# One DMA transpose for the probabilities of a pair of units instead of two, in a block-sparse attention with a feed-forward layer

## The chip, the core and the metric

The kernel runs on one core of one Trainium2 chip. The metric is the time of one execution on the device in microseconds (us); lower is better. A core has TensorE (PE in the profile, with its weight loads as PEld), VectorE (DVE), ScalarE (ACT), GpSimd (POOL) and SyncE (SP). SP computes nothing: it is the engine that issues this kernel's DMAs, one after the other in program order. Sixteen DMA engines then move the data.

## The reference

Attention over 4 batches, 8 heads, 768 positions and a head size of 64, with a mask of 32x32 blocks; then one feed-forward layer over the 3072 tokens.

```
scores = q @ k^T / sqrt(64)                       # [4, 8, 768, 768]
mask   = |block_i - block_j| <= 1, or block_i or block_j is the first or last block,
         or block_j is one of three sampled blocks of block_i
attn   = softmax(where(mask, scores, -1e9))
x      = (attn @ v) as [3072, 512]
h      = x @ w_in                                 # [3072, 2048]
out    = max(0.01 * h, h) @ w_out                 # [3072, 512]
```

## The kernel before

**Tiling.** Two blocks of queries (64 rows) make a tile `T`; there are 12 tiles in a batch. Only the keys that the mask allows are gathered: 12 slots of 32 keys, so 384 keys (`KEYS`) for a tile. A *unit* is one tile with two heads (64 query rows of the one and of the other fill the 128 partitions); a *pair* is two units with neighbouring `hp`, so four heads of one tile. Tile 0 of each batch (the first and the last query block) sees all 768 keys, and its units have two `parts` of 384 keys; all other units have one. That makes 192 units, 96 pairs and 208 parts. Four tiles (256 tokens) make an *item*, and once an item's attention is done its feed-forward layer runs in 8 chunks: `ffn_h` (lines 739 to 751, matmuls at L749), the leaky ReLU on ACT, DVE and POOL (L756, L760, L765, L766) and `ffn_o` (L768 to 784, matmuls at L779). TensorE multiplies in fp16; values are split into a high and a low half, and products are summed over halves.

**One unit.** `scores` (L651) multiplies queries and gathered keys into PSUM; `unit_ttr` (L658, DVE) adds the mask and takes the row's extreme; `unit_exp` (L669, ACT) makes the exponentials in a float32 buffer `p`. `pair_norm` (L677, L678) makes the two reciprocals `r` of a pair. `unit_high` (L684, ACT) writes the high half of the probabilities to a buffer `pp`, `unit_split` writes the low half (L689, DVE) and has SP transpose the buffer by a DMA into `pt` (L692). `pair_av` (L714) multiplies both units' `pt` with the values into `av`; it takes the pair's second unit first. `pp` and `pt` each have six buffers of one part; a counter (`tlive`) makes `split_step` emit a pair's `pair_av` before a seventh `pt` would be needed.

**The queue.** All DMAs are issued by SP: queries (`rq`), their transpose (L535, `qs`) and the exchange of its halves (L537, L538, `qxs`), keys (`rk`) and their transpose (L512, `kt`, a buffer of 128x1536 fp16 elements that comes out as 12 blocks of 128x128), values, the scratch copy of the values (`scr`), and for each tile the gather of its values into one of two buffers `vg` (L611 to L621: six of the rows' addresses are read by SP itself from a table, L619). `pt<-pp` transposes 128x768 elements, 6 blocks; `qs<-qa` 128x1024, 8 blocks.

**What sets the order.** The loop over `units` (L1027 to 1126) emits the steps with priorities; a scheduler then lays all engines' instructions out by its own model of their times and of when buffers come free. Each engine executes its list strictly in that order and waits on semaphores where data or a buffer is not ready. So a change to one instruction moves others all over the program.

Of the kernel before, what the change touches and what calls it, by code (L numbers as in the profile page):

```python
# [11 lines left out]
F16 = mybir.dt.float16  # L12
# [7 lines left out]
P = 128  # L20
# [8 lines left out]
KEYS = SLOTS * BLOCK  # L29
CFG = {  # L30
    "ahead": 3,
    "av_lag": 3,
    "bs": 1500,
    "early": 2,
    "flag": 1,
    "g": 2,
    "g_at": 0,
    "ht": 1,
# [5 lines left out]
    "ob": 4,  # L44
    "ord": "dtsixScmgovabphw",
    "p": 4,
    "pp": 6,
    "pt": 6,
    "rq": 1,
    "q_at": 8,  # L50
    "rk": 2,
# [14 lines left out]
def tile_block_sparse_attention_ffn(  # L66
# [19 lines left out]
    nc = tc.nc  # L86
# [13 lines left out]
    NCH = KEYS // P  # L100
# [6 lines left out]
    pa = ctx.enter_context(tc.tile_pool(name="pa", bufs=2))  # L107
# [571 lines left out]

    def unit_high(u):  # L680
        u.r = u.pair.r[:, u.pi:u.pi + 1]
        u.pp = [pa.tile([P, 2, KEYS], F16, tag="pp", name=f"pp_{u.nm}_{i}", bufs=CFG["pp"]) for i in range(u.parts)]
        for p, pp in zip(u.p, u.pp):
            nc.scalar.activation(pp[:, 0, :], p, AF.Copy, scale=u.r)  # L684

    def unit_split(u):
        u.pt = []
        for i, (p, pp) in enumerate(zip(u.p, u.pp)):
            nc.vector.scalar_tensor_tensor(  # L689
                out=pp[:, 1, :], in0=p, scalar=u.r, in1=pp[:, 0, :], op0=ALU.mult, op1=ALU.subtract)  # L690
            pt = pa.tile([P, 2, NCH, P], F16, tag="pt", name=f"pt_{u.nm}_{i}", bufs=CFG["pt"])
            nc.sync.dma_start_transpose(  # L692
                out=pt.rearrange("p l c t -> p (l c) t"), in_=pp.rearrange("p l t -> p (l t)"))
            u.pt.append(pt)

    avs = {}

    def pair_av(pr):

        if pr.hp == 0:  # L700
            avs[pr.item.n, pr.T] = bank(f"av_{pr.nm}", "av").rearrange("p (n l t) -> p n l t", n=NP, l=2)
        pr.av = avs[pr.item.n, pr.T]
        for u in pr.units:
            require_v(u.b, u.hp, u.T)
        emits = []
        for u in pr.units[::-1]:
            n = NCH * u.parts
            for c in range(n):
                for l in range(2):
                    for hh in range(2):  # L710
                        vt = vgs[u.b, u.T][:, c, 2 * u.hp + hh, :] if u.T else v16s[u.b, u.hp][:, c, hh, :]
                        emits.append(lambda o=pr.av[hh * D:(hh + 1) * D, u.hp], a=vt[:, l * D:(l + 1) * D],
                                     m=u.pt[c // NCH][:, :, c % NCH, hh * D:(hh + 1) * D], c=c, l=l, n=n:
                                     nc.tensor.matmul(o, a, m, start=(c == 0 and l == 0), stop=(c == n - 1 and l == 1)))  # L714
        together(emits)

    def tile_evac(pr):

        it = pr.item
        tmp = pf.tile([P, NP, Q2], F32, tag="avt", name=f"avt_{pr.nm}", bufs=1)  # L720
        nc.scalar.activation(tmp, pr.av[:, :, 1, :], AF.Copy, scale=1.0 / PSCALE)
        yield
        xf = pf.tile([P, NP, Q2], F32, tag="xf", name=f"xf_{pr.nm}", bufs=1)
        nc.vector.scalar_tensor_tensor(
            out=xf, in0=pr.av[:, :, 0, :], scalar=1.0 / PSCALE, in1=tmp, op0=ALU.mult, op1=ALU.add)
        yield
        if it.x is None:
            it.x = pa.tile([P, 2, NP, N2], F16, tag="x", name=f"x_{it.nm}", bufs=CFG["xbufs"])
        xs = it.x[:, :, :, pr.k * Q2:(pr.k + 1) * Q2]
        nc.scalar.activation(xs[:, 0], xf, AF.Copy)  # L730
        yield
        nc.gpsimd.tensor_tensor(out=xs[:, 1], in0=xf, in1=xs[:, 0], op=ALU.subtract)  # L732
        it.nx += 1
# [78 lines left out]
    for b in range(B):  # L812
        for j in range(NI):
# [3 lines left out]
            for k_ in range(TPI):  # L817
                for hp in range(0, NP, 2):
                    pr = Unit()
                    pr.item, pr.k, pr.T, pr.hp, pr.nm, pr.units = it, k_, j * TPI + k_, hp, f"{it.nm}_{k_}_{hp}", []  # L820
                    for pi in range(2):
                        u = Unit()
# [171 lines left out]
    def high_step():  # L994
        if pend_high:
            unit_high(pend_high[0])
            pend_split.append(pend_high.popleft())

    tlive = [0]

    def split_step():
        if pend_split:
            pu = pend_split.popleft()
            while tlive[0] + pu.parts > CFG["pt"]:
                av_step(True)
            tlive[0] += pu.parts
            unit_split(pu)
            live[0] -= pu.parts
            if pu.pi == 1:
                pend_av.append((step + CFG["av_lag"], pu.pair))  # L1010

    def av_step(now=False):
        if pend_av and (now or pend_av[0][0] <= step):
            pr = pend_av.popleft()[1]
            tlive[0] -= 2 * pr.units[0].parts
            while evs and pr.hp == 0:
                ev_step()
            pair_av(pr)
            if pr.hp == NP - 2:
                vfree[0] += pr.T > 0  # L1020
                evs.append(tile_evac(pr))

    def ev_step():
        if evs and next(evs[0], "end") == "end":
            evs.pop(0)

    for u in units:  # L1027
# [9 lines left out]
        if nb < B:  # L1037
            g = it.j * 16 + ui
            t = g - (CFG["k_at"] if b else CFG["k_at0"])
# [5 lines left out]
            t = g - CFG["v_at"]  # L1045
# [17 lines left out]
        c = aq[0] if aq else None  # L1063
        for w in CFG["ord"]:
# [19 lines left out]
            elif w == "t":  # L1084
                while live[0] + u.parts > CFG["p"]:
                    if not pend_high and not pend_split:
                        norm_step()
                    high_step()
                    split_step()
# [6 lines left out]
            elif w == "d":  # L1096
                norm_step()
            elif w == "i":
                high_step()
            elif w == "s":  # L1100
                split_step()
            elif w == "a":
                av_step()
                if vq and vfree[0] and (vq[0][0], "ready") in scr:
                    start_gather_v()
            elif w == "v":
                ev_step()
            elif w == "b":
                do_out()
            elif w == "o":  # L1110
                do_o(CFG["flag"] if hq or aq else 0)
            elif w == "p":
                side_step(CFG["side0"] if step < 16 else CFG["side"])
                gather_step(2)
            elif w == "w":
                wcredit += [r for a, r in CFG["wr"] if step >= a][-1]
                while wcredit >= 1.0:
                    c = next(weights, "end")
                    wcredit -= c if c != "end" else wcredit
            elif w == "h":  # L1120
                for i in range(n):
                    if i:
                        do_act()
                        do_o(CFG["flag"])
                    do_h()
# [3 lines left out]
    while pend_norm or pend_high or pend_split or pend_av or evs:  # L1129
        ev_step()  # L1130
        av_step()
        split_step()
        norm_step()
        high_step()
        if step in ready:
            add_ffn(ready.pop(step))
        do_h()
        do_act()
        do_o(CFG["flag"])
        do_out()  # L1140
        step += 1
# [49 lines left out]
```

## Time and profile before

| what | value |
|---|---|
| time before, median of 3 runs | 943.82 us (943.46 to 947.15) |
| the profiled execution, first to last instruction | 944.7 us |
| TensorE, share of the span busy | 80% |
| DVE, ACT, POOL | 64%, 52%, 35% |
| mean granted TensorE clock | 0.931 of full speed |
| DMA issues of `pt<-pp` | 208 |

The profile is of one execution, and its span stands for that execution's own time: 0.9 us above the median of the runs. The execution has four stages. Up to 60 us the inputs and the first weights arrive; from 60 to 213 us the weights are decoded and split while the first attention units run; from 213 to about 860 us attention and feed-forward chunks run side by side; after 860 us the last items' feed-forward layers are left. The views name a line as L714 and a DMA as `pt<-pp` (what it writes and reads). SP's instructions are sequencer instructions: the profile has their start and length, and counts no busy time for the engine.

### The profile page before, as it was taken

How to read it: one execution, taken by the hardware profiler on the slowest of the kernel's cores; microseconds unless marked ns; L12 is line 12 of the kernel's file. 1: busy time of each engine (PE TensorE's matmuls, PEld its weight loads, DVE VectorE, ACT ScalarE, POOL GpSimd, SP SyncE). 2: the span in 40 equal slices, each digit the busy share in tenths (PEclk: the TensorE clock that was granted, in tenths of full speed). 3: DMA queues.
4: the chain of work that ended last, by engine and by line, in shares of the span. 5: the costliest groups of instructions: out<-in, count | busy, mean ns of one | idle time of the engine just before them, and what ended most of it. 6: DMA issues, size and time to landing. Idle time of an engine off the chain costs nothing. (4 is left out here: it accounts for less than half of the span.)

```text
span 944.7 us, 21784 instructions
## 1 busy us (share of the span) xinstructions
PE 754.8 (80%) x7020; PEld 492.8 (52%) x7020; DVE 609.1 (64%) x1643; ACT 488.1 (52%) x1063; POOL 331.3 (35%) x469
## 2 busy tenths in 40 slices
PE   1325456788978979979897968989888988989998
PEld 1214334465645645646554635556455655656674
DVE  4989899996857667557565565567466655745221
ACT  4565768575535456456455554456355554535121
POOL 0234665542215344243324242333323433532221
PEclk9998557799989989999999998999999999989999
DMA  9996798678685767766675978676785665555200
GB/s 209 283 276 162 162 244 187 164 148 167 141 180 128 160 121 157 160 137 130 151 165 111 171 134 147 151 146 127 151 161 125 137 136 139 120 113 123 32 23 23
DMA packets 336624, 139.38 MB, mean 148 GB/s; under 512 B 299389, under 2 KB 311678, under 8 KB 336510
## 3 DMA queue, kind: packets, MB, share of 16 engines
q1 hardware_dynamic: 336510, 137.99, 68.5%
q8 instruction: 55, 0.90, 0.4%
q14 instruction: 59, 0.48, 0.2%
HBM read 65.57 MB, written 12.58 MB: 83 GB/s over the span
## 5 line engine op out<-in xcount | busy, mean ns | idle before, releaser
L779 PE MATMUL o<-W,g 128*128 128x512 f16 x1152 | 279.1, 388 | 7.6 <-ACT ob L797 2.9
L749 PE MATMUL h<-x,W 128*128 128x256 f16 x2304 | 280.9, 279 | 0.3 <-DVE ht L760 0.3
L749 PEld LDWEIGHTS <-W 128*128 128x128 f16 x2304 | 227.2, 101 | 50.7 <-issue 10.5
L766 POOL TENSOR_TENSOR g<-ht,g 128x512 f16<-128x512 f32 x96 | 115.3, 1201 | 336.5 <-DVE g L765 201.2
L689 DVE SCALAR_TENSOR_TENSOR pp<-p,r,pp 128x384 f16<-128x384 f32 x208 | 142.5, 702 | 106.0 <-ACT pp L684 104.4
L779 PEld LDWEIGHTS <-g 128*128 128x128 f16 x1152 | 108.8, 100 | 137.4 <-issue 23.9
L669 ACT ACTIVATE p<-p,mx 128x384 f32<-128x384 f32 x208 | 125.8, 606 | 96.3 <-DVE mx L658 67.0
L591 POOL COPY kg<-kt 128x256 f16 x264 | 129.3, 510 | 131.6 <-PE s L651 74.9
L684 ACT ACTIVATE pp<-p,r 128x384 f16<-128x384 f32 x208 | 119.6, 607 | 103.9 <-DMA pt<-pp 72.0
L714 PE MATMUL av<-pt,vg 128*64 128x128 f16 x2112 | 83.0, 231 | 50.5 <-DMA pt<-pp 40.3
L658 DVE CUSTOM_DVE_ANT_0 p<-s,em,nsc 128x384 f32<-128x384 f32 x176 | 101.9, 609 | 21.1 <-PE s L651 20.0
L714 PEld LDWEIGHTS <-vg 128*64 128x64 f16 x2112 | 72.1, 116 | 77.0 <-issue 57.4
L760 DVE SCALAR_TENSOR_TENSOR ht<-h,gd,ht 128x512 f32<-128x512 f32 x80 | 59.8, 747 | 56.0 <-ACT ht L756 55.7
L756 ACT ACTIVATE ht<-h,gs 128x512 f32<-128x512 f32 x80 | 54.0, 675 | 63.9 <-PE h L749 48.7
L651 PE MATMUL s<-kg,qs_q 128*64 128x384 f16 x352 | 65.1, 364 | 12.1 <-DVE mx L658 7.7
L732 POOL TENSOR_TENSOR x<-xf,x 128x256 f16<-128x256 f32 x48 | 35.8, 745 | 90.7 <-ACT x L730 90.0
L651 PE MATMUL s<-kg,qxs_q 128*64 128x384 f16 x352 | 63.9, 357 | 4.3 <-DMA qxs_q<-qs_q 4.3
L651 PEld LDWEIGHTS <-qs_q 128*64 128x64 f16 x416 | 27.9, 116 | 68.7 <-issue 45.4
L523 ACT ACTIVATE qa_q<-rq 128x512 f16<-128x512 f32 x25 | 15.7, 628 | 68.9 <-DMA rq<-in_q_dram 68.9
L765 DVE CAST g<-ht 128x512 f16<-128x512 f32 x96 | 43.4, 452 | 8.9 <-PE o L779 7.5
L677 DVE TENSOR_SCALAR sum<-sum 128x2 f32<-128x2 f32 x96 | 24.9, 259 | 37.1 <-ACT p L669 36.1
L669 ACT ACTIVATION_READ_ACCUMULATOR p<-p,mx 128x1 f32 x208 | 38.9, 187 | 0.0
(126 smaller groups left out, 726.0 us busy)
## 6 DMA issues: line engine op xcount, KB each, us to landing
vg<-scr SPq DMA_DIRECT2D x280, 64.0 KB, 1.9
vg<-scr SPq DMA_DIRECT2D x44, 256.0 KB, 3.1
v<-in_v_dram SPq DMA_DIRECT2D x32, 192.0 KB, 3.4
qxs_q<-qs_q SPq DMA_DIRECT2D x48, 128.0 KB, 3.0
scr<-v SPq DMA_DIRECT2D x16, 384.0 KB, 3.7
W<-in_moe_w_in_dram SPq DMA_DIRECT2D x5, 1024.0 KB, 5.9
rq<-in_q_dram SPq DMA_DIRECT2D x20, 256.0 KB, 3.5
out_dram<-ob SPq DMA_DIRECT2D x20, 256.0 KB, 2.3
```

The costliest lines, as they stand in the source:

```text
L591: nc.gpsimd.tensor_copy(out=kg[:, :, slot * BLOCK:(slot + 1) * BLOCK], in_=kt[:, :, bass.ds(off, BLOCK)])
L651: nc.tensor.matmul(o, a, k, start=(n == 0), stop=(n == 1)))
L658: nc.vector.tensor_tensor_reduce(out=u.p[i], in0=u.sp[i], in1=kgs[u.b, u.T][1] if u.T else zero.to_broadcast([P, KEYS]), scale=u.nsc, scal ...
L669: nc.scalar.activation(u.p[i], u.p[i], AF.Exp, scale=-1.0, bias=u.mx[:, :1], accum_out=u.pair.sum[:, u.pi, i:i + 1])
L684: nc.scalar.activation(pp[:, 0, :], p, AF.Copy, scale=u.r)
L689: nc.vector.scalar_tensor_tensor(out=pp[:, 1, :], in0=p, scalar=u.r, in1=pp[:, 0, :], op0=ALU.mult, op1=ALU.subtract)
L714: nc.tensor.matmul(o, a, m, start=(c == 0 and l == 0), stop=(c == n - 1 and l == 1)))
L749: nc.tensor.matmul(c.ph[:, i], w, x, start=(d == 0 and m == 0), stop=(d == NP - 1 and m == 2)))
L756: nc.scalar.activation(c.t, c.ph, AF.Copy, scale=scale[1])
L760: nc.vector.scalar_tensor_tensor(out=c.t, in0=c.ph, scalar=scale[0], in1=c.t, op0=ALU.mult, op1=ALU.max)
L766: nc.gpsimd.tensor_tensor(out=c.g[:, 1], in0=c.t, in1=c.g[:, 0], op=ALU.subtract)
L779: nc.tensor.matmul(o, a, w, start=(c.first and i == 0 and m == 0), stop=(c.last and i == 1 and m == 2)))
```

## The change

A pair gets one buffer `pp` that holds both units' probabilities (or, for tile 0, one unit its two parts), and one `pt`; the number of buffers falls from six of one size to three of twice the size. The low half is still written by one DVE instruction for each part, but the DMA is issued only once, after the pair's second unit (or, for tile 0, after the unit's second part), and transposes 128x1536 elements. The counter of `pt` buffers counts by the new size. Everything else in the source is the same. In the built program 208 transposes `pt<-pp` of 6 blocks become 104 of 12 blocks.

```diff
-    "pp": 6,
-    "pt": 6,
+    "pp": 3,
+    "pt": 3,
...
     def unit_high(u):
         u.r = u.pair.r[:, u.pi:u.pi + 1]
-        u.pp = [pa.tile([P, 2, KEYS], F16, tag="pp", name=f"pp_{u.nm}_{i}", bufs=CFG["pp"]) for i in range(u.parts)]
+        if u.parts == 2 or u.pi == 0:
+            u.pair.pp = pa.tile([P, 2, 2, KEYS], F16, tag="pp", name=f"pp_{u.nm}", bufs=CFG["pp"])
+        u.pp = [u.pair.pp[:, i if u.parts == 2 else u.pi] for i in range(u.parts)]
+        u.pp2 = u.pair.pp
         for p, pp in zip(u.p, u.pp):
             nc.scalar.activation(pp[:, 0, :], p, AF.Copy, scale=u.r)
 
     def unit_split(u):
-        u.pt = []
-        for i, (p, pp) in enumerate(zip(u.p, u.pp)):
+        for p, pp in zip(u.p, u.pp):
             nc.vector.scalar_tensor_tensor(
                 out=pp[:, 1, :], in0=p, scalar=u.r, in1=pp[:, 0, :], op0=ALU.mult, op1=ALU.subtract)
-            pt = pa.tile([P, 2, NCH, P], F16, tag="pt", name=f"pt_{u.nm}_{i}", bufs=CFG["pt"])
-            nc.sync.dma_start_transpose(
-                out=pt.rearrange("p l c t -> p (l c) t"), in_=pp.rearrange("p l t -> p (l t)"))
-            u.pt.append(pt)
+        if u.parts == 1 and u.pi == 0:
+            return
+        pt = pa.tile([P, 2, 2, NCH, P], F16, tag="pt", name=f"pt_{u.nm}", bufs=CFG["pt"])
+        nc.sync.dma_start_transpose(
+            out=pt.rearrange("p a l c t -> p (a l c) t"), in_=u.pp2.rearrange("p a l t -> p (a l t)"))
+        if u.parts == 2:
+            u.pt = [pt[:, 0], pt[:, 1]]
+        else:
+            for w in u.pair.units:
+                w.pt = [pt[:, w.pi]]
```

In `split_step` and `av_step` the counter `tlive` goes up by one for each new buffer and down by the pair's number of parts, where it counted parts before.

How the built programs differ is shown at two places, around the pair of units `2_2_0` and `2_2_1` of the third item of batch 1. The names are buffers with their unit (`pt_2_2_1` belongs to the third item, its third tile, unit 1) and a number of the program's own. First SP's list before; this stretch is what SP does from 670.6 to 679.3 us in the profile:

```order
L535 DMA_TRANSPOSE qs_q_0_0_8266<-qa_q_0_0_7938 128x8x128
L473 DMA rq_0_1_8271<-in_q_dram 128x8x64
L692 DMA_TRANSPOSE pt_2_2_0_0_8277<-pp_2_2_0_0_8173 128x6x128
L537 DMA qxs_q_0_0_8268<-qs_q_0_0_8266 64x1024
L538 DMA qxs_q_0_0_8268<-qs_q_0_0_8266 64x1024
L453 DMA scr_8209<-v_2_0_7644 128x6x256
L692 DMA_TRANSPOSE pt_2_2_1_0_8354<-pp_2_2_1_0_8279 128x6x128
L692 DMA_TRANSPOSE pt_2_2_2_0_8391<-pp_2_2_2_0_8356 128x6x128
```

And SP's list now, at the same place:

```order
L535 DMA_TRANSPOSE qs_q_0_0_8122<-qa_q_0_0_7797 128x8x128
L473 DMA rq_0_1_8127<-in_q_dram 128x8x64
L696 DMA_TRANSPOSE pt_2_2_1_8207<-pp_2_2_0_8029 128x12x128
L537 DMA qxs_q_0_0_8124<-qs_q_0_0_8122 64x1024
L538 DMA qxs_q_0_0_8124<-qs_q_0_0_8122 64x1024
L619 TENSOR_LOAD offs
L619 ISA x2
L619 TENSOR_LOAD offs
L619 ISA x2
L453 DMA scr_8065<-v_2_1_8213 128x6x256
L696 DMA_TRANSPOSE pt_2_2_3_8394<-pp_2_2_2_8209 128x12x128
```

The pair's one transpose stands where the first unit's stood, and the second unit's is gone from behind the copies of `qxs` and `scr`; the next transpose already serves the next pair. ACT's list at the same pair before (`ht` and `ob` are feed-forward work, `v` is the next batch's values):

```order
L684 ACTIVATE pp_2_2_0_0_8173<-p_2_2_0_0_7927,r_2_2_0_8164 128x384
L446 ACTIVATE v_2_3_8705<-v_3_7503,v_s 128x6x2x64
L684 ACTIVATE pp_2_2_1_0_8279<-p_2_2_1_0_7988,r_2_2_0_8164 128x384
L756 ACTIVATE ht_1_2_8294<-h_1_2_8231,gs_2841 128x512
L797 ACTIVATE ob_0_0_8199<-o_0_0_0_6878,beta_all 128x512
```

And now:

```order
L687 ACTIVATE pp_2_2_0_8029<-p_2_2_0_0_7786,r_2_2_0_8020 128x384
L687 ACTIVATE pp_2_2_0_8029<-p_2_2_1_0_7847,r_2_2_0_8020 128x384
L446 ACTIVATE v_2_3_8549<-v_3_7371,v_s 128x6x2x64
L764 ACTIVATE ht_1_0_8033<-h_1_0_7995,gs_2793 128x512
L729 ACTIVATE avt_2_0_2_8051<-av_2_0_0_7757 128x256
```

The two high halves of a pair now stand next to each other and write one buffer, where the copy of the values stood between them.

More of the change, by code (lines that the diff above doesn't have):

```diff
@@ L1003, in split_step @@
             pu = pend_split.popleft()
-            while tlive[0] + pu.parts > CFG["pt"]:
-                av_step(True)
-            tlive[0] += pu.parts
+            if pu.parts == 2 or pu.pi == 0:
+                while tlive[0] + 1 > CFG["pt"]:
+                    av_step(True)
+                tlive[0] += 1
             unit_split(pu)
@@ L1014, in av_step @@
             pr = pend_av.popleft()[1]
-            tlive[0] -= 2 * pr.units[0].parts
+            tlive[0] -= pr.units[0].parts
             while evs and pr.hp == 0:
```

## The prediction

> **What bounds the kernel now.** I began with the busy times and the stages.
>
> ```profile
> span 944.7 us, 21784 instructions
> ...
> core 0: us, PE busy (x) PEld busy (x) DVE busy (x) ACT busy (x) POOL busy (x), PEclk, DMA share, GB/s
> ...
> 60.00:213.00 153.00, 97.01 (x983) 66.78 (x983) 141.74 (x355) 100.24 (x204) 78.72 (x87) 0.75 0.82 178
> 213.00:860.00 647.00, 564.32 (x5337) 363.58 (x5331) 403.52 (x1116) 333.11 (x765) 221.44 (x346) 0.96 0.69 143
> 860.00:945.00 85.00, 80.87 (x646) 53.95 (x644) 23.40 (x49) 19.18 (x36) 18.19 (x17) 0.99 0.21 43
> ```
>
> From 60 to 213 us DVE is busy for 141.74 of 153 us: it decodes weights, and at most 11 us can be won there. From 213 to 860 us no computing engine is full. PE comes nearest with 564.3 of 647 us, and leaves 82.7 us idle. The last 85 us are feed-forward work on a PE that is 95% busy. So the question is what makes PE wait for 82.7 us in the long stage; its own list of waits there says it (who waited, for what: us in total, times, longest):
>
> ```profile
> PE av L714 <- DMA pt<-pp: 36.5, 22, 4.5
> PE k_sum L126 <- ACT k_k L494: 20.8, 7, 4.9
> PE s L651 <- DMA qxs_q<-qs_q: 7.5, 5, 2.6
> ...
> PE s L651 <- DMA qs_q<-qa_q: 2.9, 3, 1.6
> ...
> ACT pp L684 <- DMA pt<-pp: 72.0, 33, 6.8
> ...
> ACT k_k L494 <- DMA kt<-k_k: 26.0, 7, 8.5
> ```
>
> The last two rows are ACT's in the same stage. The second row's wait for ACT is itself a wait for a DMA: ACT's `k_k` stands behind the transpose of the keys, which frees the buffer. So 36.5 + 20.8 + 7.5 + 2.9 = 67.7 of PE's 82.7 us end with a DMA that SP issues. Is such a DMA late because it moves slowly, or because it is issued late? SP's own timeline answers (start, length; x counts instructions in a row):
>
> ```profile
> 668.50 0.36 SPq L804 DMA_DIRECT2D out_dram<-ob  x1
> 668.92 0.41 SPq L805 DMA_DIRECT2D out_dram<-ob  x1
> 669.38 0.53 SPq L806 DMA_DIRECT2D out_dram<-ob  x1
> 670.00 0.53 SPq L808 DMA_DIRECT2D out_dram<-ob  x1
> 670.63 1.34 SPq L535 DMA_TRANSPOSE qs_q<-qa_q  x1
> 672.02 0.57 SPq L473 DMA_DIRECT2D rq<-in_q_dram  x1
> 672.64 1.33 SPq L692 DMA_TRANSPOSE pt<-pp  x1
> 674.16 0.48 SPq L537 DMA_DIRECT2D qxs_q<-qs_q  x1
> 674.68 0.59 SPq L538 DMA_DIRECT2D qxs_q<-qs_q  x1
> 675.32 0.59 SPq L453 DMA_DIRECT2D scr<-v  x1
> 676.01 3.24 SPq L692 DMA_TRANSPOSE pt<-pp  x2
> ```
>
> Each instruction begins some 0.05 us after the one before it has ended: SP never rests. The semaphore waits in front of its DMAs confirm it (the rows give lengths in ns, min/median/max; transposes L692 of both stages, then the gather L621):
>
> ```profile
> L692 SPq DMA_TRANSPOSE pt<-pp x40: 1210/1240/3559, 59.7 to 209.6; - x40
> ...
> L692 SPq DMA_TRANSPOSE pt<-pp x168: 1209/1252/2463, 225.0 to 877.6; - x168
> L692 SPq EVENT_SEMAPHORE  x139: 17/17/670, 231.5 to 877.6; - x139
> ...
> L621 SPq EVENT_SEMAPHORE  x70: 17/17/17, 106.0 to 871.1; - x70
> ```
>
> A wait of 17 ns is no wait. Whenever SP reaches a transpose, its data has long been there, and whenever it reaches a gather, the buffer is free. SP is the late one, up to its last transpose at 877.6 us. How late, two counts up to 650 us show:
>
> ```profile
> L689 DVE SCALAR_TENSOR_TENSOR pp<-p,r,pp x148: 594/618/2475, 53.0 to 648.0; 128x384 f16<-128x384 f32 x148
> ...
> L692 SPq DMA_TRANSPOSE pt<-pp x143: 1210/1252/3559, 59.7 to 643.8; - x143
> ```
>
> DVE has written 148 parts, SP has sent off 143. Five parts at 647 us / 168 = 3.85 us each are some 19 us of lag, and with six `pp` buffers that is also what makes ACT wait 72.0 us for one to come free. One view speaks against this reading, the list of SP's waits:
>
> ```profile
> SPq L692 <- PE h L749: 11.2, 14, 1.5
> ```
>
> It puts about 0.8 us before some transposes, ended by engines that have nothing to do with them. That list infers waits from semaphore events, and such a length fits inside the transpose's own 1.25 us, so I go by the recorded lengths. The kernel is then bound, from 60 to 877 us, by the time SP takes to issue, with DVE (60 to 213 us) and PE (after) close behind.
>
> **The change part by part.** *Fewer issues.* 208 transposes of 6 blocks go, 104 of 12 blocks come. The trace has transposes of exactly that size, those of the keys, and one of 8 blocks (lengths in ns; then the median us from issue to landing):
>
> ```profile
> L512 SPq DMA_TRANSPOSE kt<-k_k x12: 1429/1462/2496, 213.9 to 617.1; - x12
> ...
> L535 SPq DMA_TRANSPOSE qs_q<-qa_q x24: 1247/1285/2577, 13.9 to 839.5; - x24
> ...
> pt<-pp SPq DMA_TRANSPOSE x208, 3.0
> ...
> kt<-k_k SPq DMA_TRANSPOSE x12, 4.1
> ```
>
> 6, 8 and 12 blocks take SP 1.252, 1.285 and 1.462 us: nearly all of it is fixed. By medians SP is spared 40 x 1.240 - 20 x 1.462 = 20.4 us before 213 us, and 168 x 1.252 - 84 x 1.462 = 87.5 us after it, 108 us in all, without the short semaphore instructions. If nothing else bound, the end would come 108 us earlier.
>
> *What that is worth.* Before 213 us nothing: DVE's 93% is the cover (bound: 11 us). After it PE is next. Its 36.5 us for `pt` go whole, because the longest of these waits, 4.5 us, is a fraction of the lag that caused them. Of the other 31.2 us (keys and queries) I take half, 15.6: those DMAs leave earlier as well, but part of their wait is their own landing, here 4.1 us for the keys.
>
> *Later landing.* One transpose of a pair lands 4.1 us after its issue, where the second of two in a row landed 1.25 + 3.0 = 4.3 us after the first one's issue. Back to back nothing is lost. Where the two stood apart (`qxs` and `scr` stood between them above), the pair's data is there 1.1 us later after the last issue than now. At all 22 places where PE waited for `pt` that is 24 us, at none 0; with the lag shrinking I charge a third, 8 us.
>
> *Buffers.* Three of double size hold as much as six. The first unit's half comes free only with the second's, and its transpose is not sent alone; while SP is 19 us behind that costs nothing. ACT's second high half of a pair loses its wait for a DMA of its own. The DMA engines move the same bytes, at a share of 0.69 in this stage; PE, DVE and ACT keep their work, and the reshuffled order of the program is charged at nothing, as the trace prices none of it (a few us either way).
>
> *Sum.* 36.5 + 15.6 - 8 = 44 us. 944.7 - 44 = 900.6 us for the profiled execution, which is 0.9 us above the median of the runs: **900 us**. PE would then be busy for 564.3 of 603 us in the long stage, 94%, a little less than the 95% of the last one. SP's last transpose could leave at 877.6 - 108 = 770 us, while PE's pace puts it near 835 us: SP would no longer set the pace.
>
> *A rule against it.* SP's record says that issuing is what runs out. The Trainium skill ("DMA: Bandwidth & Descriptors", section "Issuing engines are not separate DMA queues") says that the sequencer's time to start a DMA is usually small relative to the DMA itself. By that rule sparing issues would save next to nothing and the sum would be 944; the trace differs, with 1.25 us of issue in the 3.0 us to landing.
>
> **The rivals.**
> - *Issuing only looks full.* SP runs ahead with gathers and loads that are not urgent, and what PE waits for is the landing. Then 944 us. For it: the DMA share of 0.69. Against it: 17 ns waits everywhere and five parts of lag; SP is not ahead of anything. This is also the way in which the change would do nothing. The rule of the page named above leads to this case.
> - *Half of it.* SP is relieved, but ACT and DVE, which feed each other in strict order for every unit, take over, and only half the `pt` waits go: 944 - 18 = 926 us. For it: ACT's 72 us of waits for buffers are replaced by waits along the chain ACT to DVE to ACT. Against it: both are busy for little over half the stage.
> - *More than that.* All 67.7 us go, and DVE's 11 us: 944 - 79 = 865 us. Against it: PE would be 97% busy in strict order.
> - *Slower: the ring of buffers.* A pair's buffer comes back as one, 4.1 us after its issue, where the first unit's came back after 3.0 us. If this round trip, not SP, sets ACT's pace, 84 pairs x 1.1 us = 92 us are added on ACT; at the rate at which ACT's 72.0 us stand beside PE's 36.5 that is 47 us on PE. Set against the 36.5 us won, 954 us. It decides once over three quarters of the pairs find no free buffer (64 x 1.1 x 0.51 = 36 us); now 33 of 168 writes wait.
>
> **How the numbers follow.** About 0.5%, 4.7 us, is what a measurement of this kernel can tell from no change. Chances: forecast (880 to 918 us) 0.60, half of it (918 to 939) 0.19, more (below 880) 0.10, no change (939 to 949) 0.06, slower 0.05. Faster: 0.89. The range leaves out the last two and a part of the ends: 870 to 932 us.
>
> **What would show it.** Right: 104 rows of 12 blocks at about 1.46 us on SP; its last transpose well before 877 us; semaphore waits in front of SP's DMAs that now last microseconds; PE's wait for `pt` under 15 us and ACT's under 30. Wrong: transposes at 2.5 us each (issue grows with the blocks, no gain); SP still without a pause and the end unmoved; or ACT's wait for `pp` above 72 us, which is the slower case. What could make the forecast miss most is the new order of the whole program, which I could not price.

## The result and the profile after

| | before | after |
|---|---|---|
| time, median of 4 runs each | 943.66 us (943.46 to 947.15) | 902.65 us (900.72 to 906.05) |
| ratio | 1 | 0.956 (95%: 0.954 to 0.959) |
| profiled execution, first to last instruction | 944.7 us | 902.0 us |
| mean granted TensorE clock | 0.931 | 0.941 |
| last `pt<-pp` leaves SP at | 877.6 us | 831.6 us |

The page's busy times after:

```profile
span 902.0 us, 21419 instructions
...
PE 741.3 (82%) x7020; PEld 485.8 (54%) x7020; DVE 619.6 (69%) x1643; ACT 487.2 (54%) x1063; POOL 329.2 (37%) x469
```

And its windows (PE, PEld, DVE, ACT and POOL busy, with instructions; then clock, DMA share and GB/s), cut where the long stage now ends (818 us):

```profile
60.00:213.00 153.00, 89.20 (x911) 60.14 (x911) 138.19 (x340) 95.87 (x192) 69.08 (x84) 0.78 0.75 175
213.00:818.00 605.00, 559.40 (x5413) 364.26 (x5411) 418.19 (x1137) 338.19 (x782) 228.28 (x348) 0.97 0.72 154
818.00:902.00 84.00, 80.08 (x637) 52.87 (x634) 22.03 (x41) 17.81 (x32) 18.20 (x17) 1.00 0.19 39
```

The cuts at 60 and 213 us are those of before; between them PE does 911 matmuls where it did 983. The last stage takes 84 us where it took 85. The long one takes 605 us where it took 647, and PE's idle time in it falls from 82.7 to 45.6 us. What PE and ACT wait for there (us in total, times, longest):

```profile
PE s L651 <- DVE mx L658: 12.5, 6, 3.8
PE av L722 <- DMA pt<-pp: 7.2, 4, 3.9
PE s L651 <- DMA kt<-k_k: 6.9, 1, 6.9
PE s L651 <- DMA qxs_q<-qs_q: 6.0, 4, 2.4
PE k_sum L126 <- ACT k_k L494: 5.9, 5, 2.3
PE s L651 <- DMA qs_q<-qa_q: 3.3, 2, 2.2
...
ACT p L669 <- DVE mx L658: 70.4, 44, 8.6
...
ACT pp L687 <- DMA pt<-pp: 23.3, 10, 4.5
```

PE's wait for `pt` went from 36.5 to 7.2 us, ACT's wait for a `pp` buffer from 72.0 to 23.3 us. ACT's largest wait is now that for DVE's `mx`. It is not new; the rows of the kernel before, from 213 to 860 us, were

```profile
PE s L651 <- DVE mx L658: 4.4, 5, 1.3
...
ACT p L669 <- DVE mx L658: 57.2, 42, 5.8
```

Now SP's own rows, of its transposes with their landing, and of the gather's address reads:

```profile
L696 SPq DMA_TRANSPOSE pt<-pp x104: 1406/1674/4695, 59.1 to 831.6; - x104
L696 SPq EVENT_SEMAPHORE  x87: 17/17/631, 58.7 to 831.5; - x87
...
DMA to landing us min/median/max: 3.6/4.1/7.1
```

```profile
L619 SPq TENSOR_LOAD <-offs x264: 262/276/1097, 25.4 to 828.8; - x132
```

The landing is the forecast 4.1 us. The issue is not the forecast 1.462 us but 1.674, and the waits ahead of it are still 17 ns. SP sent its last transpose at 831.6 us, not at 770.

### The profile page after: what moved, and what is told of

Same layout as the page of the kernel before. It is cut to its first block, busy times and chain, and to the rows that moved or that the text cites. A ratio compares the mean times of both kernels' runs of the same rounds, so it can differ in the third digit from the quotient of the medians.

```text
span 902.0 us, 21419 instructions
## 1 busy us (share of the span) xinstructions
PE 741.3 (82%) x7020; PEld 485.8 (54%) x7020; DVE 619.6 (69%) x1643; ACT 487.2 (54%) x1063; POOL 329.2 (37%) x469
## 5 line engine op out<-in xcount | busy, mean ns | idle before, releaser
L787 PE MATMUL o<-W,g 128*128 128x512 f16 x1152 | 275.1, 384 | 5.7 <-DVE g L773 3.3
L591 POOL COPY kg<-kt 128x256 f16 x264 | 124.0, 488 | 179.1 <-PE s L651 100.9
L687 ACT ACTIVATE pp<-p,r 128x384 f16<-128x384 f32 x208 | 115.5, 607 | 63.6 <-DMA pt<-pp 23.7
L722 PEld LDWEIGHTS <-vg 128*64 128x64 f16 x2112 | 71.1, 114 | 42.0 <-issue 37.1
L677 DVE TENSOR_SCALAR sum<-sum 128x2 f32<-128x2 f32 x96 | 32.4, 337 | 37.4 <-ACT p L669 36.9
L651 PE MATMUL s<-kt,qs_q 128*64 128x384 f16 x64 | 12.8, 394 | 33.1 <-DVE mx L658 17.1
```

The costliest lines, as they stand in the source:

```text
L591: nc.gpsimd.tensor_copy(out=kg[:, :, slot * BLOCK:(slot + 1) * BLOCK], in_=kt[:, :, bass.ds(off, BLOCK)])
L651: nc.tensor.matmul(o, a, k, start=(n == 0), stop=(n == 1)))
L787: nc.tensor.matmul(o, a, w, start=(c.first and i == 0 and m == 0), stop=(c.last and i == 1 and m == 2)))
```

## The experiments

Three questions were open: whether issuing was the cause at all, whether SP still sets the pace, and where about half of the 108 us that SP should have been spared went. Each ratio below is to runs of the kernel before that were made beside the experiment; there it stood at 946.3 to 946.7 us.

**1. The pair's buffers, but two issues** (changed kernel).

```diff
-        nc.sync.dma_start_transpose(out=pt..., in_=u.pp2...)          # 12 blocks
+        for a in range(2):
+            nc.sync.dma_start_transpose(out=pt[:, a]..., in_=u.pp2[:, a]...)   # 6 blocks each
```

> The kernel after, but each pair's transpose is split into two of 6 blocks, issued one right behind the other at the pair's end; the shared buffers, the writes into them and the wait for both units stay. Theory A (the gain is SP's issue time): the second issue costs SP about 1.25 us for each of 104 pairs and gives back most of what was saved, 930 to 950 us, and the queue's last transpose leaves at 865 us or later. Rival B (the gain comes from the shared buffer: one wait instead of two for ACT, both units released and landed together): 900 to 910 us.

Measured: 949.73 us (946.76 to 954.05), ratio to before 1.0036 (1.0012 to 1.0061). The whole gain is gone, and SP is as late again as before:

```profile
L697 SPq DMA_TRANSPOSE pt<-pp x208: 1210/1254/4313, 60.6 to 883.7; - x104
```

So the gain comes from the single issue, and the buffers of a pair bring nothing by themselves. PE's waits from 213 to 860 us in this run hold a warning:

```profile
PE k_sum L126 <- ACT k_k L494: 14.6, 6, 3.3
PE s L651 <- DMA qxs_q<-qs_q: 13.8, 7, 2.8
...
PE av L723 <- DMA pt<-pp: 10.8, 10, 1.9
PE s L651 <- DMA qs_q<-qa_q: 9.9, 4, 3.3
```

PE waits only 10.8 us for `pt` here, where the kernel before had 36.5, and yet the time is no better: PE is idle for 77.6 us of this stage (82.7 before), and other rows have grown in its place, those of the queries (`qs`, `qxs`) from 10.4 to 23.7 us above all. The size of one row of waits is not what its DMA costs.

**2. SP's time given back as something else** (changed kernel, plus one read of the address table, whose value is not used, behind each transpose; dependencies that the cut below leaves out hold the read and its bounds steps behind their transpose, and the next transpose behind them).

```diff
         nc.sync.dma_start_transpose(...)
+        nc.sync.value_load(offs[:1, :1], min_val=0, max_val=S - BLOCK)
```

> The kernel after, with one table read more on SP behind each of the 104 transposes. It moves no data and nobody waits for it; it only costs SP about 0.28 + 0.15 + 0.02 us and the pauses between, some 0.5 us, 52 us in all. Theory A (SP still sets the pace after the change): 940 to 958 us. Rival C (as the prediction had it: after the change SP has slack and PE sets the pace): 903 to 915 us.

Measured: 962.38 us (958.77 to 964.52), ratio to before 1.0179 (1.0137 to 1.022), 4 us above the range. The 104 reads move no data that anyone waits for, and cost 60 us against the changed kernel. SP's last transpose leaves 61 us later:

```profile
L697 SPq DMA_TRANSPOSE pt<-pp x104: 1403/1515/4522, 58.9 to 893.0; - x104
...
L699 SPq TENSOR_LOAD <-offs x104: 269/960/1249, 63.5 to 894.5; - x104
```

A read behind a transpose takes 0.960 us where those of the gather took 0.276 (medians). The transposes themselves read shorter (1.515 against 1.674 us). Part of what a transpose of 12 blocks costs SP thus stands in the row of the next instruction. Summed over SP's records and usual pauses from 60 us to the last transpose, SP has 797 us to do instead of 731 in the changed kernel: 67 us more, for 60 us of time. Part of the loss lies before 213 us, where DVE is busy for 126.5 us instead of 138.2; how much of that is due to the order that the dependencies force was not separated. Taken as a whole, added time on SP still counts nearly in full after the change.

**3. Another order, nothing else** (kernel before, one number of the table that sets the order).

```diff
-    "bs": 1500,
+    "bs": 1300,
```

> The kernel before with one number of the priorities changed (the lead of the scaling steps, 1500 to 1300): the same work, buffers and DMAs, but a new order on all engines. Theory A (the reshuffled order is worth little): 936 to 952 us. Rival D (a new order alone can be worth what the change brought): 20 us or more away from 944 us, either way.

Measured: 955.48 us (953.13 to 960.14), ratio 1.0105 (1.0052 to 1.0157), 3 us above the range. The window from 60 to 213 us shows where 10 us could lie:

```profile
60.00:213.00 153.00, 88.82 (x859) 59.00 (x859) 131.22 (x310) 93.43 (x189) 70.31 (x81) 0.72 0.75 178
```

DVE is busy for 131.22 us there, 10.5 us less than in the kernel before, in the stage in which it is the fullest engine. This agrees with the loss; it was not tried by itself. One other order cost 1% here, so differences of 1% between kernels whose order differs are not evidence of anything else.

**4. The price of a transpose alone.** This kernel leaves out the whole computation: SP issues transposes of 3, 6, 12 and 24 blocks of 128x128, first each one followed by table reads, then four in a row.

```diff
+    for word, n in {"three": 3, "six": 6, "twelve": 12, "twentyfour": 24}.items():
+        for i in range(4):
+            transpose(n, f"lone_{word}_{i}_"); read(f"then_{word}", 1); read("rest", 15)
+    # ... then four in a row: row_{word}
```

> The attention and the feed-forward layer are left out; SP only issues transposes of 3, 6, 12 and 24 blocks, alone with one table read behind and then rest, and four in a row. Theory T (a transpose goes on costing SP after its own record ends, by its number of blocks): the read behind takes about 0.35, 0.6, 0.95 and 1.6 us where a read at rest takes 0.27, and four of 12 blocks in a row take 1.7 us each, not 1.46. Rival F (the record is the whole price): 0.27 us behind each, and 1.25 and 1.46 us in a row for 6 and 12 blocks.

The reads, at rest and right behind a transpose (ns, min/median/max), and transposes in a row:

```profile
L97 SPq TENSOR_LOAD <-rest x364: 262/263/999, 2.5 to 290.7; - x182
L97 SPq TENSOR_LOAD <-then_three x4: 329/344/348, 6.5 to 37.8; - x4
L97 SPq TENSOR_LOAD <-then_six x4: 579/582/591, 48.5 to 80.6; - x4
L97 SPq TENSOR_LOAD <-then_twelve x4: 879/974/987, 91.3 to 125.3; - x4
L97 SPq TENSOR_LOAD <-then_twentyfour x4: 753/860/974, 139.0 to 179.2; - x4
...
L91 SPq DMA_TRANSPOSE row_six__2722<-src x1: 1281/1281/1281, 212.4 to 212.4; - x1
...
L91 SPq DMA_TRANSPOSE row_twelve__2998<-src x1: 1298/1298/1298, 234.0 to 234.0; - x1
L91 SPq DMA_TRANSPOSE row_twelve__3000<-src x1: 1967/1967/1967, 235.3 to 235.3; - x1
L91 SPq DMA_TRANSPOSE row_twelve__3002<-src x1: 1798/1798/1798, 237.3 to 237.3; - x1
...
L91 SPq DMA_TRANSPOSE row_twentyfour__3280<-src x1: 3703/3703/3703, 266.0 to 266.0; - x1
```

The record of a transpose of 12 blocks with no transpose right ahead of it looks cheap (1.298 us here); the rest of its price, 974 - 263 = 711 ns, is in the next instruction, or in the next transpose. Behind 3, 6 and 12 blocks the read came as theory T had it. Behind 24 blocks it takes 0.860 us and not 1.6: there most of the price is in the record itself. In a row 6 blocks take 1.28 us, 12 about 1.81 and 24 about 3.70: about 0.15 us for each block of the larger ones, while even 3 blocks take 1.25 us. Two transposes of 6 blocks cost 2 x 1.28 = 2.56 us and one of 12 costs 1.81, so a pair saves 0.75 us where SP is full and not 2 x 1.252 - 1.462 = 1.04: 78 us for 104 pairs, not 108. Two of 12 blocks (3.62 us) and one of 24 (3.70) cost the same: by these rows, which are of one execution, merging further would spare SP nothing.

**5 and 6. No address reads at all** (the kernel before, and the changed one; the sampled blocks are gathered from fixed rows instead of the table's, so the output is of other keys' values; the dependencies that kept the reads in order go with them).

```diff
-            off = nc.sync.value_load(offs[:1, i:i + 1], min_val=0, max_val=S - BLOCK)
+            off = i * BLOCK % S
```

> The kernel before, but SP gathers values from fixed rows instead of the sampled blocks: the same DMAs and bytes without SP's 264 table reads and register steps, some 200 us of SP's time. Theory A (SP sets the pace before): 870 to 895 us, and SP's semaphore waits grow beyond 17 ns. Rival G (a smaller number of transposes has a worth of its own, in landing or buffers): little of it, 925 to 945 us, because there are still 208 transposes.

> The kernel after with the same fixed gather. Theory A: with SP's time no longer short, merging the transposes is worth little, so 865 to 890 us and within 10 us of the fixed gather with 208 transposes. Rival G: some 40 us below that kernel, as between the two kernels of the case.

Measured: 871.75 us (869.32 to 878.43; ratio 0.9213, 0.9158 to 0.9268) and 858.26 us (854.61 to 863.61; ratio 0.9045, 0.9005 to 0.9086). SP's transposes and the window of the long stage (PE's busy time and matmuls come first), of the kernel before with fixed rows:

```profile
L691 SPq DMA_TRANSPOSE pt<-pp x208: 1209/1229/4013, 58.7 to 800.0; - x104
```

```profile
213.00:820.00 607.00, 577.43 (x5633) 378.83 (x5633) 423.82 (x1143) 341.51 (x784) 235.00 (x353) 0.99 0.79 154
```

and of the changed one:

```profile
L695 SPq DMA_TRANSPOSE pt<-pp x104: 1394/1489/5147, 59.9 to 790.2; - x104
```

```profile
213.00:820.00 607.00, 586.39 (x5725) 386.06 (x5724) 428.48 (x1151) 346.60 (x791) 237.45 (x355) 0.99 0.76 155
```

Without touching a transpose, the kernel before gains 75 us (946.65 us in the same comparison), more than the change. Number 5 came in its range; number 6 came 7 us below its range, and 13.5 us below number 5 where at most 10 were expected. With SP relieved in this way the change is worth 871.75 - 858.26 = 13.5 us, a third of the 41 us with all reads in place. PE is then 95% and 97% busy: it comes nearest to being the bound.

**7 and 8. A part of SP's issues moved to ACT** (loads of values, most key loads, scratch copies, output stores; kernel before and changed kernel).

```diff
-            nc.sync.dma_start(out=t[:, :, h, :], in_=v[b, 2 * hp + h]...)
+            nc.scalar.dma_start(out=t[:, :, h, :], in_=v[b, 2 * hp + h]...)
   ... the same for scr, the k loads of batches 1 to 3, and out
```

> The kernel before, with the loads of values and later keys, the copies to scratch and the stores of the output issued by ACT instead of SP: about 70 us of SP's time go to an engine that is 52% busy; transposes and gathers stay as they were. Theory A (SP sets the pace): 880 to 915 us. Rival H (what counts is the transposes): 940 to 950 us; above 950 us if ACT's waits for these DMAs' buffers cost more than SP saves.

> The kernel after with the same DMAs moved to ACT. Theory A (SP still sets the pace after the change, as the added table reads showed): 870 to 892 us. Rival C (PE sets the pace after the change): 895 to 905 us. Above 905 us if ACT pays more than SP saves.

Measured: 939.27 us (936.02 to 946.73; ratio 0.9929, 0.9888 to 0.997) and 905.68 us (904.42 to 910.16; ratio 0.9574, 0.9534 to 0.9615). Both missed, by 24 us and 14 us beyond their ranges; 7 stands at the edge of its rival's 940 to 950 us, and 8 just above its rival's 895 to 905. Counted as in the table below, SP had 37 us less to do from 60 us on in 7 than in the kernel before, and rested 30 us more, and yet only 4 to 7 us were won: less work on SP is not enough by itself. In both the first transpose left later than in the unmoved kernels (at 71.6 and 73.0 us, by 12 and 14 us), so a late start was the suspicion, and experiment 11 tried it for the changed kernel.

**9, 10 and 12. Cheaper address reads, with the right addresses.** One instruction reads a tile's six addresses and the steps that check their bounds are left out (9: changed kernel, 10: kernel before); or the single reads stay and only the steps go (12: changed kernel).

```diff
-            off = nc.sync.value_load(offs[:1, i:i + 1], min_val=0, max_val=S - BLOCK)
+        _, offv = nc.values_load_multi_w_load_instructions(offs[:1, i0:i0 + 2 * NR],
+            engines=[SP], min_val=0, max_val=S - BLOCK, skip_runtime_bounds_check_because=...)
```

> Changed kernel, but SP reads a tile's six row addresses with one instruction in place of six and leaves out the steps that check their bounds: 264 reads become 44, the addresses are the same. Theory (SP's issue time still sets the pace of the changed kernel): what SP is spared, about 94 us of single reads less 44 longer ones and the checks behind each, comes off until PE is full: 855 to 875 us, near the 858 us with no reads at all, and PE over 95% busy from 213 to 820 us. Rival (after the change SP no longer sets the pace, PE's own work and the order of the steps do): 895 to 905 us, and SP shows real pauses in front of its transposes.

> The kernel before with the same edit alone, two transposes for a pair as ever. Theory (both edits draw on one budget, SP's time): 865 to 890 us, so this edit alone is worth more than the change, and with it the change is worth only 10 to 25 us more instead of 43. Rival (the two gains are independent): the change is worth 40 us here as well, so this kernel stands about 40 us above the changed one with the same edit.

> Changed kernel, with the 264 single reads kept but the steps that check their bounds left out. SP is spared a part of what one read for a tile spares it. Theory (the time follows SP's time): 870 to 895 us, between the changed kernel and the one with one read for a tile. Rival (only the reads' own wait for memory, not SP's total time, counts, since the reads hold up the gathers): no change, 898 to 906 us.

Measured: 884.97 us (882.58 to 888.04; ratio 0.9333, 0.9304 to 0.9363), 922.50 us (915.86 to 925.99; ratio 0.9723, 0.9669 to 0.9777) and 881.28 us (874.52 to 883.41; ratio 0.9284, 0.9235 to 0.9334). So 12 came in its range, though not above 9 as expected (their intervals overlap); 9 missed by 10 us and gained about half of what was expected; and 10 missed by 32 us. Numbers 9 and 12 beat both kernels of the case. That the time falls with SP's time holds in all three; that it follows down to the level without reads does not. In 9, SP's list of waits between 213 and 820 us shows why, and below it stands the row of the semaphore instructions ahead of the same gather:

```profile
SPq L611 <- PE av L727: 62.0, 17, 5.4
```

```profile
L611 SPq EVENT_SEMAPHORE  x41: 17/17/17, 71.3 to 803.1; - x41
```

SP now stands in front of the gather until PE has done with a buffer of `vg`. It is ahead of PE there, and PE is busy for 569.27 of the 607 us (94%, not over 95% as expected). These rows hold a trap as well: the gather's semaphore instructions still last 17 ns while SP stands idle for up to 5.4 us. SP's timeline at one of those places:

```profile
573.18 3.87 SPq L701 DMA_TRANSPOSE pt<-pp  x2
582.05 0.38 SPq L611 DMA_DIRECT2D vg<-scr  x1
```

The semaphore's record of 17 ns stands at 577.1 us, behind the transposes; from there to 582.05 us, where the gather's DMA begins, SP has no record at all. A wait can thus be an empty stretch between the semaphore's record and that of the DMA instead of a long record. Whether SP rests must be read from the gaps. I added up all gaps between SP's records above 0.15 us (without the usual 45 ns of each) and all semaphore records above 0.06 us, from 213 us to the last transpose:

| kernel | SP at rest | of | time |
|---|---|---|---|
| before | 10.6 us | 665 us | 943.7 us |
| after | 19.6 us | 619 us | 902.7 us |
| 10: before, one read | 51.9 us | 639 us | 922.5 us |
| 12: after, no bound steps | 74.3 us | 596 us | 881.3 us |
| 9: after, one read | 100.5 us | 602 us | 885.0 us |
| 5: before, no reads | 71.5 us | 587 us | 871.8 us |
| 6: after, no reads | 138.5 us | 577 us | 858.3 us |
| 8: after, DMAs on ACT | 46.4 us | 619 us | 905.7 us |

SP is full before (98%) and after (97%), and only the edits beyond the change give it rest. Once SP has rest, more of it no longer means less time: 9 rests more than 12 and is no faster, and 8 is no faster than the changed kernel. Number 10 does not fit one budget alone: SP rests for 52 us, and the time is still 922.5 us. There PE waits for the queries, 30.7 us from 213 to 820 us where the kernel before had 6.2 in these two rows and the same window:

```profile
PE s L656 <- DMA qxs_q<-qs_q: 19.6, 8, 3.5
PE s L656 <- DMA qs_q<-qa_q: 11.1, 5, 4.6
```

Before that stage, from 60 to 213 us, DVE is busy for 133.0 us where it was 141.7 in the kernel before, a loss like that of experiment 3. Why its order brings the queries late was not tried and stays open. With one read the change is worth 922.5 - 885.0 = 37.5 us, as the rival said, and not 10 to 25.

**11. As 8, but the first batch stays on SP** (of the keys the second batch too; 84 DMAs are moved where 8 moved 104).

```diff
-            nc.sync.dma_start(out=t[:, :, h, :], in_=v[b, 2 * hp + h]...)
+            (nc.scalar if b else nc.sync).dma_start(out=t[:, :, h, :], in_=v[b, 2 * hp + h]...)
```

> Changed kernel, with the loads of values and their scratch copies from the second batch on, the key loads of the last two batches and all output stores issued by ACT instead of SP; the first batch stays on SP, so that the start is not held up as in the earlier try (first transpose at 73 us instead of 59). Theory (the earlier try missed because of its delayed start; otherwise less work on SP is a gain): 875 to 895 us, first transpose again near 59 us. Rival (ACT's own issuing and its waits eat what SP wins, start or no start): 900 us or more with the start as in the changed kernel.

Measured: 911.32 us (907.23 to 913.14), ratio 0.9616 (0.9576 to 0.9655). The first transpose is at 59.3 us again, SP rests for 53.5 us after 213 us, and the kernel is no faster than the changed one. So the late start was not what kept the gain away from the changed kernel; for the kernel before (7) it was not tried. The scratch copies on ACT show what the rival named:

```profile
L453 ACTq EVENT_SEMAPHORE  x12: 17/1657/3877, 249.1 to 645.7; - x12
L453 ACTq DMA_DIRECT2D scr<-v x12: 378/392/513, 252.0 to 645.8; - x12
```

A copy waits 1.66 us at the head of ACT's list, and all the DMAs moved take 45 us of ACT's time by their records. From 60 to 213 us DVE is busy for 133.8 us here, 4.4 us less than in the changed kernel. How much of the lost gain is due to which of these was not separated.

## Why the prediction was right, and where it was wrong

**What bounds the kernel: right, with one weak reason.** SP's issue time set the pace. Giving the two issues back takes the whole gain away (1), and reads that move nothing cost 60 us (2). The Trainium skill ("DMA: Bandwidth & Descriptors", section "Issuing engines are not separate DMA queues") calls the sequencer's time to start a DMA usually small relative to the DMA itself; experiment 2 shows a kernel in which that time decides. But "a wait of 17 ns is no wait" was no good proof, as experiment 9 shows. The gaps (10.6 us of rest in 665) and the lag were. By 650 us DVE has now written 156 low halves and SP sent 76 transposes, so 152 halves: four behind, where it was five.

**The price of one issue: wrong, by half of the saving.** I took 1.462 us from the transpose of the keys, whose row leaves out what the instruction behind it pays, and expected SP to be spared 108 us. Summed over SP's records, the `pt<-pp` transposes fell from 282.9 to 192.7 us (mean 1.853 us each), so by 90.2 us. Of that, the address reads took back 13.5 us and the gathers 8.3 (L611 and L621), as experiment 4 would have it, since some of them stand behind longer transposes. SP's rests from 60 us on grew from 17.4 to 42.8 us, more than half of it before 213 us, where DVE is the fullest engine (138.19 of 153 us). The last transpose ended 879.6 - 833.3 = 46.3 us earlier (90.2 - 13.5 - 8.3 - 25.4 = 43.0, and 3.3 in other rows and pauses).

**"SP would no longer set the pace": wrong.** It rests for only 3% of the stretch from 213 us to its last transpose, which left at 831.6 us and not at 770. The semaphore waits of microseconds that the forecast named as a sign did not appear. Experiments 2, 6, 9 and 12 move its time up and down, and the kernel follows by +60, -44, -18 and -21 us (medians against 902.65; the kernel before stood 3 us higher in those comparisons).

**The sum of 44 us: close, but in part by terms that cancelled.** PE's idle time in the long stage fell by 37.1 us. Its wait for `pt` gave 29.3 of the forecast 36.5 - 8 = 28.5. This agreement is partly luck: in experiment 1 the same row is 10.8 us with none of the gain left, so the row does not measure what the late transposes cost. Keys and queries gave 31.2 - 22.1 = 9.1 of 15.6 (`k_sum` 5.9, `qxs` 6.0, `qs` 3.3 and a new 6.9 for `kt`). Against that, PE waits 12.5 us for DVE's `mx`, a row that had 4.4 before. From 60 to 213 us PE was idle 7.8 us longer, and DVE busy 3.5 us less (141.74 to 138.19): the front was not free of charge, though I had charged nothing for it. The rest of the gain was not in the forecast at all. PE's busy time before was

```profile
PE 754.8 (80%) x7020; PEld 492.8 (52%) x7020; DVE 609.1 (64%) x1643; ACT 488.1 (52%) x1063; POOL 331.3 (35%) x469
```

and 13.5 us less after: 1.8% for the same 7020 matmuls, while the mean granted clock was 1.1% higher (0.931 to 0.941). If their time goes with the clock, which no run here tried by itself, that is an estimated 8 us of the 13.5; the rest stays open. Together (idle time of the long stage, of the one from 60 to 213 us and of the others, then busy time): -37.1 + 7.8 + 0.1 - 13.5 = -42.7 us, the difference of the spans. The forecast of 900.6 us is a span, to be held against 902.0 us. It was then set beside the median of the times, although a span leaves out about 1.6 us of its execution's time (902.0 of 903.64 us after).

**The rivals.** "Issuing only looks full" fell with experiments 1 and 2. "Half of it" did not come: ACT waits for DVE's `mx` for 70 us (57 before), but PE's own wait for it is 12.5. "More than that" is not in the change itself, since SP stayed full; with SP relieved further it is reached (858 us without reads). The slower rival, the ring of buffers, did not show: ACT's wait for `pp` fell to 23.3 us.

**The new order.** Charged at nothing, "a few us either way". One change of order cost 9 us in experiment 3, and the order of experiment 10 may have cost more, so the agreement to 3 us is in part luck.

## What to carry to other kernels

Count the time of the queue that issues the DMAs as that of an engine: when it has no gaps, every instruction on it costs, the small reads of addresses too, and cheaper reads gave 18 to 21 us on top of the change. Take the price of an issue from instructions that stand in a row, or from the sum over all the queue's records, since a single row can leave part of the price to its neighbour. A saving on a full queue is worth its size only until the next engine is full: here 41 us with all reads in place and 13.5 us without them. Between these, with one read for a tile, it was still 37.5 us, though SP had rest in both kernels; the order of experiment 10 stands in the way of reading that figure.

## What the runs showed of the hardware that I had not expected

- The issue of a DMA transpose on SP costs about 1.28 us for 6 blocks of 128x128 and about 0.15 us a block for 12 and 24 blocks (1.81 and 3.70 us in a row, experiment 4). Merging 6-block transposes into one of 12 pays; by these rows merging on does not.
- Part of that price falls on the next SP instruction: a table read of 263 ns takes 582 ns behind 6 blocks, 974 ns behind 12 and 860 ns behind 24.
- A semaphore record of 17 ns can stand ahead of an idle stretch of 5 us (experiment 9): the wait is in the gap behind it.
- A read of six table values with one instruction takes SP 1.28 us (experiment 9); six single reads take 6 x 0.28 us and their bounds steps:

```profile
L621 SPq TENSOR_LOAD <-offs x44: 1270/1284/2312, 73.2 to 808.7; - x44
```
